# A hand-written opening order, y sums on TensorE and fp32 attention for a third block, in an attention and two-MoE kernel

## The chip, the cores and the metric

One core of a Trainium2 chip runs the whole kernel. The metric is device microseconds (us) from the first to the last instruction, as the median of three executions. Engines are named as the profile names them: PE is TensorE (PEld its weight loads), DVE is VectorE, ACT is ScalarE, POOL is GpSimd, and SP is the engine whose queue starts most DMAs. Each engine takes its instructions strictly in its own order and waits where one is not ready.

## The reference, cut

```python
# attention without softmax, then a dense two-layer block, then a mixture of 8 experts
kv  = einsum('bhsd,bhse->bhde', k, v)          # 8 batches, 8 heads, 576 rows, 64 columns
out = einsum('bhsd,bhde->bhse', q, kv)
x   = out / sqrt(mean(out*out, -1) + 1e-6) * g_norm      # 4608 tokens x 512
h   = x @ w_in                                           # 512 x 2048
g   = maximum(h, 0) + alpha * minimum(h, 0)
y   = g @ w_out                                          # 2048 x 512
e   = argmax(y @ w_gate, axis=1)
out = gate(y) * sigmoid(y @ w_output_gate)[e] * (relu(y @ w1[e]) @ w2[e])
```

The inputs of the dense block are 64 bits wide and are read as pairs of 32-bit words.

## The kernel before, in words

The 4608 tokens are 12 blocks of 384 (three tiles of 128). For every block there is an attention part that ends in `x`, the block's rows transposed, as an fp16 high and low part; then 16 pieces `h` (12 matmuls of 384 columns each, `h_piece`, L602), then three tiles `y` (48 matmuls of 512 columns each, `y_products`, L621). A product of split numbers is three fp16 matmuls: high by high, high by low, low by high. After each `h`, ACT scales it into `m` (L605), DVE makes `r` of it (L607), ACT writes the high half of `g` (L609) and POOL, in blocks 0 and 1, or DVE, in the later ones, the low half (L610).

The weights `wi` (of w_in) and `wo` (of w_out) are converted while blocks 0 and 1 run, in four quarters of four pieces each. A piece is a 0.5 MB load into one of five buffers, an absolute value on ACT (L454), then four DVE instructions that form an fp32 value from the two words (L455, L458, L460, L462: `build`). When a quarter's four pieces are built, a maximum over the 128 partitions is taken through two TensorE products (`all_max`, L150 and L155), a chain of small DVE instructions forms the scale (`pow2`, `scale_in`, `scale_out`), and each piece is split into a high part on ACT (L476) and a low part on DVE (L477). `h` of a quarter needs the four pieces of `wi`, `y` of a quarter the four of `wo`. Blocks 0 and 1 are therefore computed quarter by quarter (`h_part`, `y_part`), and the sums over quarters are kept in `accs` (in the buffers of `g` that are not yet in use): ACT scales the new quarter into `yt` (L660) and DVE adds it to the rescaled sum (L661).

The attention of blocks 0 and 1 is in fp32: ACT copies q (L318), PE transposes it (L321), ACT copies that to `qT` (L323), PE multiplies by `kvbd` into `ops` (L339). From block 2 on (`SPLIT_Q = 2`) q is scaled on POOL (L309), split into fp16 halves on ACT and DVE, transposed by a DMA, and multiplied by the split `kv16` (L336), whose scale comes from `kv_halves` (a scaling on POOL, L280). After `ops` the steps are the same: square (ACT, L341), sum (DVE, L343), a power on POOL (L350), an exponent by small DVE instructions (L353 to L362), scaling (DVE, L368), the high half on ACT (L372), the low half on POOL from block 2 on (L373), and a transposing DMA into `x` (L376).

The order on all engines is made by a scheduler that goes by its own estimates; only the last dense block and the expert part are pinned to the written order. After block 11 the routed rows go through the experts (L1090, L1112).

Of the kernel before, what the change touches and what calls it, by code (L numbers as in the profile page):

```python
# [20 lines left out]
P = 128  # L21
# [8 lines left out]
NG = 4  # L30
# [28 lines left out]
SPLIT_Q = 2  # L59
# [7 lines left out]
def body(ctx: ExitStack, tc, q, k, v, g_norm, w_in, w_out, alpha, w_gate, w_og, w1, w2, out):  # L67
# [60 lines left out]
    def pow2(am, nm, out_s, out_inv, top=14, wide=False):  # L128
# [111 lines left out]
    def load_kv_first():  # L240
        for nm, src, w in (("k", k, wi[:, 6:11]), ("v", v, wi[:, 11:16])):
# [3 lines left out]
            sp.dma_start(out=m, in_=src[0, :, 0:QJ * P, :].rearrange("h (p j) d -> p h j d", j=QJ))  # L245
            sp.dma_start(out=r, in_=src[0, :, QJ * P:S, :].rearrange("h p d -> p h d"))
            kv_in[nm + "r", 0] = r
            for n in range(NPAIR):
                kv_in[nm, n] = m[:, 2 * n:2 * n + 2]

    def kv_step(n):
# [19 lines left out]
    def kv_halves(b):  # L271
# [8 lines left out]
        pool.tensor_tensor(out=t, in0=src, in1=s_.unsqueeze(2).to_broadcast([P, H, D]), op=ALU.mult)  # L280
# [5 lines left out]
    def att_steps(i):  # L286
# [3 lines left out]
        split_q = i >= SPLIT_Q  # L290

        def tr(t):
# [3 lines left out]
            if split_q:  # L296
# [12 lines left out]
                pool.tensor_tensor(out=qs, in0=qv, in1=s_.unsqueeze(2).to_broadcast([P, H, D]), op=ALU.mult)  # L309
# [17 lines left out]
        def om(t):  # L327
# [987 lines left out]
```

## Time and profile before

| | |
|---|---|
| median of three runs | 1383.14 us (1381.43 to 1385.01) |
| the profiled execution | 1379.12 us |
| its span, first to last instruction | 1377.3 us |
| PE busy | 1274.2 us, 93% of the span |
| DVE busy | 837.6 us, 61% |
| ACT busy | 560.5 us, 41% |
| POOL busy | 334.0 us, 24% |
| mean granted TensorE clock | 0.965 of full speed |

Busy shares are averages over stages with different limits, so they are read by stage: the opening (blocks 0 and 1, with the weight conversion), blocks 2 to 11, and the experts. A group row gives a line of the kernel, engine, operation, what is written from what, the count, busy time and mean duration. A timeline row gives start and duration of one instruction or of several merged ones, and in brackets how long the engine had been idle and what it waited for. The granted clock has two levels, 2.4 GHz (1.0) and 1.2 GHz (0.5); a stretch's figure is a mean.

### The profile page before, as it was taken

What the parts mean: (1) busy time and instruction counts of PE and PEld (TensorE: products, weight loads), DVE (VectorE), ACT (ScalarE), POOL (GpSimd) and SP (SyncE); (2) the same over time, 40 slices, a digit from 0 to 9 for tenths busy, and PEclk for the clock granted to TensorE, in tenths of its full rate; (3) what the DMA queues carried; (4) which work ended last, traced back from release to release, by engine and by line L of the source; (5) the groups of instructions that cost most, each with busy time, mean ns of one, the idle gap of its engine ahead of it and who ended that gap; (6) DMA issues with size and microseconds to landing.
All of it is one profiled execution on the core that took longest, in us unless ns stands there. A gap on an engine that the chain in (4) does not pass through costs nothing. (4 is left out here: it accounts for less than half of the span.)

```text
span 1377.3 us, 21930 instructions
## 1 busy us (share of the span) xinstructions
PE 1274.2 (93%) x7586; PEld 659.5 (48%) x7586; DVE 837.6 (61%) x2476; ACT 560.5 (41%) x928; POOL 334.0 (24%) x410
## 2 busy tenths in 40 slices
PE   3579898899999999999999999999989999999995
PEld 2435354455555555555555555554434444444442
DVE  5989968777777887868696878562521221212210
ACT  3355553446554565655464656351111111111110
POOL 3023134332212222223231222101322221222210
PEclk9579998899999999999999999999999999999998
DMA  9944135547594867685736666316999799799641
GB/s 286 242 114 136 50 92 127 131 130 196 163 267 109 238 169 192 191 214 156 235 63 178 168 170 146 108 39 174 254 328 195 152 314 267 147 232 247 136 89 38
DMA packets 326433, 237.00 MB, mean 172 GB/s; under 512 B 249372, under 2 KB 282156, under 8 KB 321840
## 3 DMA queue, kind: packets, MB, share of 16 engines
q1 hardware_dynamic: 308144, 189.88, 55.6%
q0 software_dynamic: 8960, 28.91, 6.5%
q10 hardware_dynamic: 9216, 16.78, 3.8%
q8 instruction: 61, 1.00, 0.3%
q14 instruction: 52, 0.43, 0.1%
HBM read 248.34 MB, written 53.25 MB: 219 GB/s over the span
## 5 line engine op out<-in xcount | busy, mean ns | idle before, releaser
L602 PE MATMUL h<-x,wi 128*128 128x384 f16 x2304 | 410.3, 329 | 7.0 <-DMA x<-x 3.9
L621 PE MATMUL y<-wo,g 128*128 128x512 f16 x1728 | 408.0, 383 | 6.7 <-ACT g L609 3.5
L602 PEld LDWEIGHTS <-wi 128*128 128x128 f16 x2304 | 222.2, 98 | 163.0 <-issue 11.0
L621 PEld LDWEIGHTS <-g 128*128 128x128 f16 x1728 | 164.8, 98 | 192.9 <-issue 8.5
L1096 DVE CAST h_d<-br_d 128x512 f16<-128x512 f32 x62 | 26.7, 430 | 259.9 <-DMA hT_d<-h_d 147.3
L1112 PE MATMUL bo_d<-lane,hT_d 128*128 128x512 f16 x744 | 168.1, 383 | 7.8 <-DMA hT_d<-h_d 7.8
L1090 PE MATMUL bh_d<-lane,byT_d 128*128 128x512 f16 x744 | 165.3, 379 | 0.0
L609 ACT CAST g<-r 128x384 f16<-128x384 f32 x192 | 97.0, 508 | 113.3 <-DVE r L607 108.9
L607 DVE SCALAR_TENSOR_TENSOR r<-m,alphat 128x384 f32<-128x384 f32 x192 | 123.1, 642 | 23.5 <-ACT m L605 22.6
L1112 PEld LDWEIGHTS <-hT_d 128*128 128x128 f16 x744 | 73.0, 99 | 98.8 <-DMA hT_d<-h_d 9.3
L1090 PEld LDWEIGHTS <-byT_d 128*128 128x128 f16 x744 | 72.6, 98 | 88.1 <-issue 0.8
L350 POOL TENSOR_TENSOR rs<-ms,mhalf 128x8 f32<-128x8 f32 x36 | 67.3, 1869 | 192.8 <-DVE qm L353 192.7
L610 DVE TENSOR_TENSOR g<-r,g 128x384 f16<-128x384 f32 x160 | 91.7, 575 | 23.5 <-ACT g L609 22.8
L605 ACT ACTIVATE m<-h,scal 128x384 f32<-128x384 f32 x160 | 91.5, 574 | 27.8 <-PE h L602 26.5
L412 DVE SCALAR_TENSOR_TENSOR wlo_w<-rawe,es_w,whi_w 128x1024 f16<-128x1024 f32 x64 | 85.2, 1347 | 26.0 <-DMA ws<-wlo_w 15.8
L1094 ACT ACTIVATE br_d<-bh_d 128x512 f32<-128x512 f32 x62 | 37.0, 597 | 131.6 <-PE bh_d L1090 109.2
L763 POOL DMA_INDIRECT ytab<-row,pos x36 | 37.9, 1052 | 215.8 <-DVE pos L744 110.4
L542 ACT ACTIVATE eab_w<-rawe 128x1024 bf16<-128x1024 f32 x64 | 67.0, 1055 | 56.7 <-DMA rawe<-in_moe_w_dram 47.1
L411 ACT ACTIVATE whi_w<-rawe,es_w 128x1024 f16<-128x1024 f32 x64 | 71.3, 1144 | 31.9 <-DVE es_w L142 19.6
L1116 POOL DMA_INDIRECT out_dram<-ob_d,oidx_d x31 | 32.3, 1041 | 192.8 <-ACT ob_d L1115 192.8
L1115 ACT ACTIVATE ob_d<-bo_d,msc_d 128x512 f32<-128x512 f32 x31 | 21.3, 687 | 140.8 <-PE bo_d L1112 140.8
L373 POOL TENSOR_TENSOR x<-xs,x 128x512 f16<-128x512 f32 x30 | 37.2, 1241 | 105.0 <-ACT x L372 79.2
(363 smaller groups left out, 1366.7 us busy)
## 6 DMA issues: line engine op xcount, KB each, us to landing
lane<-ws SPq DMA_DIRECT2D x150, 1024.0 KB
rawe<-in_moe_w_dram SPq DMA_DIRECT2D x64, 512.0 KB
ws<-whi_w ACTq DMA_DIRECT2D x64, 256.0 KB
ws<-wlo_w SPq DMA_DIRECT2D x64, 256.0 KB
q<-in_q_dram SPq DMA_DIRECT2D x16, 512.0 KB
rawwi<-in_moe_w_in_dram SPq DMA_DIRECT2D x16, 512.0 KB
rawwo<-in_moe_w_out_dram SPq DMA_DIRECT2D x16, 512.0 KB
k<-in_k_dram SPq DMA_DIRECT2D x28, 256.0 KB
```

The lines of the kernel that those rows point to most:

```text
L350: pool.tensor_tensor(out=rs, in0=ms, in1=mhalf, op=ALU.pow)
L411: act.activation(out=dst_h, in_=src, func=AF.Copy, scale=s)
L412: dve.scalar_tensor_tensor(out=dst_l, in0=src, scalar=s, in1=dst_h, op0=ALU.mult, op1=ALU.subtract)
L542: act.activation(out=ab.rearrange("p a b -> p (a b)"), in_=raws[4 * m + i], func=AF.Abs)
L602: pe.matmul(ps, wi[:, f // 4 * NC + c, w, fs], xt[i][:, xc, :], start=(n == 0), stop=(n == 3 * NC - 1))
L605: act.activation(out=r0, in_=ps, func=AF.Copy, scale=(scst if start else scal)[:, f:f + 1])
L607: dve.scalar_tensor_tensor(out=r, in0=r0, scalar=alphat[:, f:f + 1], in1=r0, op0=ALU.mult, op1=ALU.max)
L609: act.copy(out=hi, in_=r)
L610: (pool if start else dve).tensor_tensor(out=lo, in0=r, in1=hi, op=ALU.subtract)
L621: pe.matmul(ps, g[:, t, f % GF, us], wo[:, f, w, :], start=(start and m == 0), stop=(stop and m == 2))
L1090: pe.matmul(hp[ts], j["yT"][:, x, ts], w1_[:, w, c, hs], start=(m == 0), stop=(m == 3 * NC - 1))
L1112: pe.matmul(po[ts], hT[:, g, ts], w2_[:, w, f, :], start=(m == 0), stop=(m == 3 * NFE - 1))
```

## The change

The first two blocks, up to the last `h` of block 1, stand in one hand-written order, pinned on PE, DVE, ACT and SP; before, the scheduler ordered them. `build` is cut into `magnitude` (ACT), `maximum` and `bits` (DVE) so that the pieces can be placed one by one. Each engine's rows before and after, at three places, follow the diff.

The sums of y over quarters move to TensorE: the old sum is multiplied by `keep`, a scaled identity in fp32, into the same PSUM tile (`y_unit`), and ACT copies the result out. The third block's attention takes the fp32 path (`SPLIT_Q = 3`), so `kv_halves` of batches 0 and 1 falls away. The copy of q is gone: PE transposes straight from the loaded tile, half a tile at a time. Three POOL steps go to DVE in all later blocks too: the scaling of q, of kv, and the low half of `x`. The early `kvbd` copies go from DVE to ACT. Maxima of one column need one DVE instruction less, the four small parameter loads start on ACT's queue, and the first k and v come in halves.

```diff
-SPLIT_Q = 2
+SPLIT_Q = 3
...
+    def max_rows(ps, n, nm):
         m = small.tile([E, 1], F32, tag="amrow", name="amrow" + nm)
         dve.tensor_reduce(out=m[:n], in_=ps[:n, 0:P], axis=AX.X, op=ALU.max)
+        if n == 1:
+            pe.matmul(ps[:, P:P + 1], ones32[:1, :], m[:1], start=True, stop=True)
+            return ps[:, P:P + 1]
...
-                dve.tensor_copy(out=kvbd[b % 2][sl, hp - 1:hp + 1, sl], in_=ps[sl])
+                (act.copy if b < 2 else dve.tensor_copy)(out=kvbd[b % 2][sl, hp - 1:hp + 1, sl], in_=ps[sl])
...
-        pool.tensor_tensor(out=t, in0=src, in1=s_.unsqueeze(2).to_broadcast([P, H, D]), op=ALU.mult)
+        dve.tensor_tensor(out=t, in0=src, in1=s_.unsqueeze(2).to_broadcast([P, H, D]), op=ALU.mult)
...
-                pool.tensor_tensor(out=qs, in0=qv, in1=s_.unsqueeze(2).to_broadcast([P, H, D]), op=ALU.mult)
+                dve.tensor_tensor(out=qs, in0=qv, in1=s_.unsqueeze(2).to_broadcast([P, H, D]), op=ALU.mult)
...
-                qj = scratch[(1, 2, 0, 3, 4, 5)[t]]
-                act.copy(out=qj.rearrange("p (h d) -> p h d", h=H), in_=qv)
-                qps = ps_a.tile([P, NPAIR, P], F32, tag="a", name="qps" + nm)
+                qps = (pool_ or ps_a).tile([P, NPAIR, P], F32, tag=tag, name="qps" + nm)
                 for hp in range(NPAIR):
-                    pe.transpose(qps[:, hp, :], qj[:, hp * P:(hp + 1) * P], ident)
+                    for e in range(2):
+                        pe.matmul(qps[64 * e:64 * e + 64, hp, :], qv[:, 2 * hp + e, :], ident, start=True, stop=True)
...
-            (dve if i < 2 else pool).tensor_tensor(out=x16[:, 1, :], in0=xs, in1=x16[:, 0, :], op=ALU.subtract)
+            tiles[t] = xs, x16
+
+        def low(t):
+            xs, x16 = tiles.pop(t)
+            dve.tensor_tensor(out=x16[:, 1, :], in0=xs, in1=x16[:, 0, :], op=ALU.subtract)
...
-            exp_to(ya[:, js], d[:, 0:1], 127 << 23)
-            exp_to(yb[:, js], d[:, 1:2], 127 << 23)
+            exp_to(d[:, 1:2], d[:, 1:2], 127 << 23)
+            act.activation(out=keep, in_=ident, func=AF.Copy, scale=d[:, 1:2])
...
+    def y_unit(i, j, g, acc, u):
+        ps = ps_y.tile([P, DM], F32, tag="y", name=f"y_{i}_{j}_{u}")
+        if j:
+            pe.matmul(ps, keep, acc[:, u, :], start=True, stop=False)
         for f in range(j * GF, (j + 1) * GF):
...
-                act.activation(out=t, in_=ps, func=AF.Copy, scale=ya[:, j:j + 1])
-                dve.scalar_tensor_tensor(out=acc[:, u, :], in0=acc[:, u, :], scalar=yb[:, j:j + 1], in1=t,
-                                         op0=ALU.mult, op1=ALU.add)
...
+        act.copy(out=acc[:, u, :], in_=ps)
...
+    with tc.manual_schedule(engines={ET.PE, ET.DVE, ET.Activation, ET.SP}):
+        load_kv_first(0)
...
+        din.magnitude(GF)
+        emit("i10 y000 i11 y001 i12 h100 i13 h101 r100 i14 h102 r101 i15 h103 r102 i16 y002 r103 i17 y100 i18 y101 o10 "
+             "y102 o11")
+        for j in range(1, NG):
+            emit(f"h0{j}0 o{j}2 h0{j}1 r0{j}0 o{j}3 h0{j}2 r0{j}1 o{j}4 h0{j}3 o{j}5 r0{j}2 h1{j}0 r0{j}3 o{j}6 h1{j}1 "
+                 f"r1{j}0 o{j}7 h1{j}2 r1{j}1 o{j}8 h1{j}3 r1{j}2")
...
+    for i in range(2):
+        for u in range(TB):
+            y_unit(i, NG - 1, gts[i], accs[i], u)
```

In the plan strings, `h0{j}x` is a piece of `h` of block 0 in quarter j, `r0{j}x` its `r` and `g`, `y0{j}u` a tile of `y`, `i` and `o` the steps of the conversion of `wi` and `wo` (0 to 3 build and take the maximum, 4 finishes the fourth piece, 5 is the second TensorE product, 6 the scale and high parts, 7 and 8 the low parts).

The first place is DVE in the first quarter, ahead of the low parts of `wi` (L477 before, L535 after). In the names, `x_0_2` is the third tile of block 0, `x_0_3` the first of block 1, `pw_ewi`, `sig`, `isig` and `scol` are the scale of `wi`. Before:

```order
L460 SCALAR_TENSOR_TENSOR cwo_1183<-rawwo_979,cwo_1183 128x512
L416 TENSOR_REDUCE amxwo_1236<-accwo_1123 128x1
L455 TENSOR_SCALAR uwi_1340,accwi_1339<-uwi_1340 128x512
L142 TENSOR_SCALAR sig<-isig 128x1
L373 TENSOR_TENSOR x_0_3_593<-xs_3_575,x_0_3_593 128x512
L486 TENSOR_TENSOR sig<-sig,sal 128x1
L487 TENSOR_TENSOR isig<-isig,ial 128x1
L488 TENSOR_TENSOR scol<-sig,gp 128x1
L132 TENSOR_SCALAR pw_ewg<-allmaxwg 128x1
L140 TENSOR_SCALAR kt<-pw_ewg 128x1
L142 TENSOR_SCALAR swg<-kt 128x1
L477 SCALAR_TENSOR_TENSOR wi<-wo,scol,wi 128x512 x2
```

After:

```order
L406 TENSOR_TENSOR x_0_1_450<-xs_1_384,x_0_1_450 128x512
L132 TENSOR_SCALAR pw_ewi_461<-allmaxwi_428 128x1
L135 TENSOR_SCALAR pw_ewi_461<-pw_ewi_461 128x1
L137 TENSOR_SCALAR sig<-pw_ewi_461 128x1
L139 TENSOR_SCALAR isig<-pw_ewi_461 128x1
L544 TENSOR_TENSOR scol<-sig,sgp 128x1
L545 TENSOR_TENSOR isig<-isig,ial 128x1
L406 TENSOR_TENSOR x_0_2_457<-xs_2_409,x_0_2_457 128x512
L508 TENSOR_SCALAR cwi_473<-uwi_402 128x512
L510 SCALAR_TENSOR_TENSOR cwi_473<-rawwi_250,cwi_473 128x512
L512 SCALAR_TENSOR_TENSOR wo<-rawwi_250,cwi_473 128x512
L535 SCALAR_TENSOR_TENSOR wi<-wo,scol,wi 128x512 x4
```

Block 1's attention and the builds of `wo` and of the second quarter of `wi` no longer stand ahead of the first low parts; the instructions of one build now follow each other directly.

The second place is the middle of the second quarter, where `y` of block 1 begins, on PE and DVE. `y_1_0` and `y_1_1` are tiles 0 and 1 of quarter 1; `allmaxwi` is the maximum for the third quarter of `wi`. PE after (before, no product by `keep` stands there):

```order
L686 MATMUL y_1_0_1312<-wo,g_200 128x512
L159 MATMUL allmaxwi_1289<-amrowwi_1327,ones_69 128x1
L711 MATMUL y_1_1_1343<-g_202,keep 128x512
L686 LDWEIGHTS g_200
L686 MATMUL y_1_1_1343<-wo,g_200 128x512
```

DVE before, in the second quarter:

```order
L477 SCALAR_TENSOR_TENSOR wo<-wi,sogs,wo 128x512
L460 SCALAR_TENSOR_TENSOR cwo_1504<-rawwo_1215,cwo_1504 128x512
L477 SCALAR_TENSOR_TENSOR wo<-wi,sogs,wo 128x512
L462 SCALAR_TENSOR_TENSOR wo<-rawwi_1187,cwi_1386 128x512
L477 SCALAR_TENSOR_TENSOR wo<-wi,sogs,wo 128x512
L152 TENSOR_REDUCE amrowwi_1412<-allmaxwi_1410 1x1
L477 SCALAR_TENSOR_TENSOR wo<-wi,sogs,wo 128x512
```

DVE after, at the third quarter's scale of `wi`:

```order
L512 SCALAR_TENSOR_TENSOR wo<-rawwi_1100,cwi_1306 128x512
L157 TENSOR_REDUCE amrowwi_1327<-allmaxwi_1289 1x1
L132 TENSOR_SCALAR pw_ewi_1330<-allmaxwi_1289 128x1
L135 TENSOR_SCALAR pw_ewi_1330<-pw_ewi_1330 128x1
L137 TENSOR_SCALAR sig<-pw_ewi_1330 128x1
L139 TENSOR_SCALAR isig<-pw_ewi_1330 128x1
L544 TENSOR_TENSOR scol<-sig,sgp 128x1
L545 TENSOR_TENSOR isig<-isig,ial 128x1
L535 SCALAR_TENSOR_TENSOR wi<-wo,scol,wi 128x512 x4
L500 TENSOR_SCALAR uwo_1341,accwo_1362<-uwo_1341 128x512
```

The scale chain now stands alone, behind a TensorE product that follows four tiles of `y`, and the low parts and the next builds stand behind it.

The third place is PE where block 2 begins. Before, the last rows of block 0's gate products (`l_2`) and its routing (`rk`) stand there, and nine rows of `rk` further on the first `h` of block 2:

```order
L697 LDWEIGHTS yT_2_2433
L697 MATMUL l_2_2468<-wg_148,yT_2_2433 128x32
L731 LDWEIGHTS tri_73
L731 MATMUL rk_2506<-oh_0_2498,tri_73 128x24
L733 LDWEIGHTS ones_71
L733 MATMUL rk_2506<-oh_0_2498,ones_71 128x16
```

After:

```order
L686 MATMUL y_3_2_2384<-wo,g_200 128x512
L273 MATMUL kvps_2_2173<-v_2_2149,k_2_2147 64x64 x8
L273 MATMUL kvps_2_2173<-vr_778,kr_774 64x64 x2
L273 MATMUL kvps_2_2173<-v_3_2168,k_3_2166 64x64 x8
L663 LDWEIGHTS wi
L663 MATMUL h_0_2405<-x_2030,wi 128x384
```

The second and third gate products and the routing of block 0 have moved behind the first pieces `h` of block 2.

## Rows read from the trace of the kernel before

**Rows 1.** Busy us (x instructions) by stretch: PE, PEld, DVE, ACT, POOL, PEclk, DMA share, GB/s

```profile
0.00:71.00 71.00, 32.77 (x287) 26.33 (x288) 51.80 (x181) 25.04 (x41) 12.52 (x54) 0.73 0.96 260
71.00:88.30 17.30, 12.05 (x62) 6.77 (x61) 15.13 (x58) 8.74 (x20) 9.09 (x8) 0.80 0.29 61
88.30:158.00 69.70, 61.58 (x299) 29.80 (x298) 68.84 (x162) 37.27 (x67) 15.23 (x13) 0.94 0.45 129
158.00:248.10 90.10, 76.65 (x503) 41.49 (x504) 71.86 (x227) 45.15 (x79) 31.51 (x28) 0.90 0.37 96
248.10:925.00 676.90, 662.30 (x4306) 360.91 (x4306) 523.23 (x1560) 369.94 (x604) 165.65 (x148) 1.00 0.61 163
925.00:1377.30 452.30, 428.81 (x2137) 194.20 (x2135) 106.73 (x293) 74.37 (x120) 100.03 (x161) 0.98 0.80 198
```

**Rows 2.** Timeline of DVE: start us, us, line, operation

```profile
15.28 0.69 DVE L455 TENSOR_SCALAR_CACHE_REDUCE uwi<-uwi 128x512 f32<-128x512 f32 x1
16.00 0.43 DVE L458 TENSOR_SCALAR cwi<-uwi 128x512 int32<-128x512 int32 x1
16.46 0.69 DVE L460 SCALAR_TENSOR_TENSOR cwi<-rawwi,cwi 128x512 int32<-128x512 int32 x1
17.07 0.68 DVE L455 TENSOR_SCALAR_CACHE_REDUCE uwi<-uwi 128x512 f32<-128x512 f32 x1
...
76.17 0.17 DVE L132 TENSOR_SCALAR pw_ekv<-allmaxkv 128x8 int32<-128x8 int32 x1 [1.60 <-PE allmaxkv L155]
76.37 0.17 DVE L140 TENSOR_SCALAR kvi<-pw_ekv 128x8 int32<-128x8 int32 x1
```

**Rows 3.** Timeline of the last v load's end on PE and of ACT, first loads

```profile
11.54 5.91 PE L262 MATMUL kvps<-wi 64*64 64x64 f32 x80 [11.54 <-DMA wi<-in_v_dram]
...
16.98 0.68 ACT L454 ACTIVATE uwi<-rawwi 128x512 f32<-128x512 f32 x1 [0.67 <-DMA rawwi<-in_moe_w_in_dram]
```

**Rows 4.** Timeline of PE, fp32 products of 128 columns (two records for each product)

```profile
19.97 1.13 PE L339 MATMUL ops<-kvbd,qT 128*128 128x128 f32 x8 [1.47 <-issue]
20.94 0.60 PE L321 MATMUL qps<-ident,g 128*128 128x128 f32 x4
...
41.23 2.08 PE L339 MATMUL ops<-kvbd,qT 128*128 128x128 f32 x8 [0.68 <-ACT qT L323]
```

**Rows 5.** Timeline where block 2's first `h` begins: SP's queue (SPq) and PE

```profile
244.79 1.24 SPq L376 DMA_TRANSPOSE x<-x  x1
...
246.36 0.20 PE L731 MATMUL rk<-oh,tri 128*128 128x24 f16 x1 [3.76 <-DVE oh L723]
...
248.09 7.00 PE L602 MATMUL h<-x,wi 128*128 128x384 f16 x24 [1.41 <-DMA x<-x]
```

**Rows 6.** Timeline of PE, `h` and `y` at the full clock

```profile
121.21 4.06 PE L602 MATMUL h<-x,wi 128*128 128x384 f16 x24
125.11 1.24 PE L621 MATMUL y<-wo,g 128*128 128x512 f16 x5
...
297.91 15.50 PE L621 MATMUL y<-wo,g 128*128 128x512 f16 x71
313.24 0.83 PE L336 MATMUL ops<-kv,qT 128*128 128x128 f16 x12
```

**Rows 7.** Timeline of POOL and DVE side by side

```profile
114.40 1.00 POOL L610 TENSOR_TENSOR g<-r,g 128x384 f16<-128x384 f32 x1 [3.94 <-ACT g L609]
114.54 1.41 DVE L460 SCALAR_TENSOR_TENSOR cwo<-rawwo,cwo 128x512 int32<-128x512 int32 x1
```

**Rows 8.** Groups of the first 248 us: the y sums on DVE

```profile
L661 DVE SCALAR_TENSOR_TENSOR g<-g,yb,yt 128x512 f32<-128x512 f32 x18 | 14.4, 800 | 6.5 <-ACT yt L660 6.5
```

**Rows 9.** Groups of the whole span on POOL

```profile
L350 POOL TENSOR_TENSOR rs<-ms,mhalf 128x8 f32<-128x8 f32 x36 | 67.3, 1869 | 192.8 <-DVE qm L353 192.7
...
L373 POOL TENSOR_TENSOR x<-xs,x 128x512 f16<-128x512 f32 x30 | 37.2, 1241 | 105.0 <-ACT x L372 79.2
L309 POOL TENSOR_TENSOR qs<-q,qsc 128x512 f32<-128x512 f32 x30 | 36.9, 1240 | 38.2 <-DVE qm L353 18.5 <-DVE qsc L142 11.8 <-DVE pw_er L132 3.6
```

More of the change, by code (lines that the diff above doesn't have):

```diff
@@ L1177, in body @@
-    prep = prep_in(0)
-    def prep_steps(n):
-        for _ in range(n):
-            if prep:
-                prep.pop(0)()
-    while prep:
-        prep_steps(1)
-        step(attq)
-        step(attq)
-    drain(attq)
-    for load in late:
-        load()
-    late = None
-    wgr = small.tile([P, NC, 2, E], F32, tag="wgr", name="wgr", bufs=1)
-    sp.dma_start(out=wgr[:, :, 0, :], in_=w_gate.rearrange("(c p) e -> p c e", p=P))
-    sp.dma_start(out=wgr[:, :, 1, :], in_=w_og.rearrange("(c p) e -> p c e", p=P))
+        load_kv_first(1)
@@ new lines, in top @@
+        def top(d, nm):
+            m = small.tile([P, 1], F32, tag="amx", name="amx" + nm)
+            dve.tensor_reduce(out=m, in_=d.acc, axis=AX.X, op=ALU.max)
+            return max_turn(m, nm, ps_l, "l")
+        (t0, t1, t2), tr, products, sums, exponents, scaled, low = att_parts(0)
+        din.magnitude(0)
+        for n in range(2):
+            kv_step(n)
+        din.build(0)
+        din.magnitude(1)
+        for n in range(2, NPAIR):
+            kv_step(n)
+        din.build(1)
@@ new lines, in body @@
+        for n in range(NPAIR, NPAIR + 2):
+            load_kv(n, True)
+        load_next()
+        tr(t0, ps_h, "h")
+        tr(t1, ps_h, "h")
+        while late:
+            late.pop(0)()
+        din.magnitude(2)
+        products(t0)
+        products(t1)
+        din.build(2)
+        tr(t2, ps_h, "h")
+        din.magnitude(3)
+        products(t2)
+        load_next()
+        sums(t0)
+        sums(t1)
+        din.maximum(3)
+        ps = top(din, "wi0")
+        sums(t2)
+        exponents(t0, t2)
@@ new lines, in body @@
+        ps = max_rows(ps, 1, "wi0")
+        scaled(t0)
+        scaled(t1)
+        low(t0)
+        scaled(t2)
+        low(t1)
+        scale_in(0, ps)
+        low(t2)
+        for i in range(3):
+            din.split(i, 0)
+        din.bits(3)
+        din.split(3, 0)
+        dout.magnitude(0)
+        load_next()
+        load_next()
+        (t3, t4, t5), tr, products, sums, exponents, scaled, low = att_parts(1)
+        tr(t3, ps_y, "y")
+        products(t3)
+        for n in range(NPAIR, NPAIR + 2):
+            kv_step(n, ps_y, "y")
@@ new lines, in body @@
+        while late:
+            late.pop(0)()
+        for i in range(GF):
+            din.split(i, 1)
+        load_next()
+        g = gts[0]
+        h0 = h_products(0, 0, True)
+        dout.build(0)
+        dout.magnitude(1)
+        h1 = h_products(0, 1, True)
+        h_unit(0, g, True, h0)
+        dout.build(1)
+        load_next()
+        dout.magnitude(2)
+        for n in range(NPAIR + 2, 2 * NPAIR):
+            kv_step(n)
+        tr(t4, ps_y, "y")
+        h_unit(1, g, True, h1)
@@ new lines, in body @@
+        h2 = h_products(0, 2, True)
+        tr(t5, ps_y, "y")
+        sums(t3)
+        dout.build(2)
+        load_next()
+        products(t4)
+        h3 = h_products(0, 3, True)
+        h_unit(2, g, True, h2)
+        dout.magnitude(3)
+        products(t5)
+        sums(t4)
+        dout.maximum(3)
+        ps = top(dout, "wo0")
+        sums(t5)
+        h_unit(3, g, True, h3)
+        exponents(t3, t5)
+        ps = max_rows(ps, 1, "wo0")
+        scaled(t3)
+        scaled(t4)
+        low(t3)
@@ L1195, in body @@
+        marks = {}
+        for ins in reversed(nc.cur_bb.bb.instructions):
+            if ins.engine in (ET.PE, ET.DVE, ET.Activation, ET.SP):
+                marks.setdefault(ins.engine, ins)
+    behind = ExitStack()
+    for ins in marks.values():
+        behind.enter_context(tc.issue_after(ins))
     gam = small.tile([P, 1], F32, tag="amx", name="gam")
```

340 lines of the change are left out of this document (204 added, 136 removed).

## The prediction

> **What bounds the kernel now.** I read the busy time by stretch first. Blocks 2 to 11 (248.1 to 925) keep PE busy for 662.3 of 676.9 us at a granted clock of 1.00, and the experts behind them 428.8 of 452.3 [rows 1]; DVE has 154 us to spare in the one and most of the other. Nothing but the 14.6 us in which PE idles can be won in blocks 2 to 11. The opening is another matter: up to 248.1 PE idles for 64.8 us (38.2, 5.2, 8.1 and 13.4 by stretch), and its granted clock is 0.73 and 0.80 up to the first `y` at 88.3. From 88.3 to 158 DVE is busy for 68.84 of 69.70 us: it sets the pace there. Ahead of it DVE shows 51.8 of 71, on a DMA share of 0.96. The timelines give three marks: the first `h` at 71.0, the first `y` at 88.3 (both are cuts of rows 1), block 2's first `h` at 248.09 [rows 5]. That `h` waited for a transposing DMA issued at 244.79, behind routing that had waited 3.76 us for DVE [rows 5]. So the sum is made of one question: when does block 2's first `h` come?
>
> **Step 1, the first h.** The change takes block 1's attention and the builds of `wo` out of DVE's queue ahead of the first low parts. One build is 0.72 + 0.46 + 0.61 + 0.69 by its starts, 2.5 us [rows 2]. The third raw block is on ACT at 16.98 [rows 3]; as much data stands ahead of it as before, the fourth lands some 3 us later. PE still gets its last v at about 11.5 and needs about 6 us for the first kv [rows 3]; transposes and products of three tiles cost four fp32 products of 128 columns each, 0.97 us at the full clock and 2.0 at half (eight records, four products, 2.08) [rows 4], so with ACT's copies between them the third tile's products end at about 29. Behind them on DVE: a sum and exponents, 2.0; a power on POOL, 1.87 [rows 9]; scalings and low parts of three tiles, about 4.5 (0.69 for a 128x512 step [rows 2]); which puts the last low part of `x` at about 38. The transposing DMA adds 3.3 (issued 244.79, usable 248.09) [rows 5]. The scale of `wi` is six small steps of about 0.2 (0.17 each and a gap) [rows 2], the fourth build 1.8, and one low part 0.69: 40.3, inside that. **The first h is at about 42** against 71.0; ends 38 (exponents hidden) and 50 (loads as late as DVE found them before).
>
> **Step 2, the first y.** What DVE was spared comes back: four builds of `wo` 10.0, block 1's three tiles 6.2 (three 0.69 steps each) with 16 small steps 2.7, four `r` 2.1 (0.69 x 384/512), the scale 1.4, four low parts 2.8; 25.2 us, and two waits for PE's maxima and ACT's high parts, 3. **70**, against 88.3.
>
> **Step 3, the quarters.** Before, 18 sums on DVE cost 14.4 us [rows 8]; they go. In their place PE gets 18 products by `keep`, fp32, 128x512. No such row exists; four times 128 columns gives 4 x 0.243 = 0.97 us at the full clock (estimate; 2.0 at half [rows 4]). That is 17.5 us more on PE, and it lies on the path wherever PE paces. From 70 PE has six `y` of 2.59 and twelve `h` of 1.95 [rows 6]: 38.9, with 2.6 for a clock not yet full 111.6. DVE has eight builds 20.0, twelve `r` 6.2, eight low parts 5.5, two scales 2.8, POOL's collisions 5.6 (below) and two waits of 2.2: 114.5. DVE is later, so quarter 1 is open to `y` at 114.5.
>
> A later quarter on PE: eight `h` 15.6 and six `y` with `keep` 6 x 3.56 = 21.4, together 37.0. On DVE it has two halves. The `o` half: three builds 7.5, the fourth's rest 1.8, four `r` 2.1, two maxima 1.1, the scale 1.7, ACT's high part 0.68, four more steps 3.2: 18.1. The `i` half does not run ahead, because its scale waits for a TensorE product that stands behind four tiles of `y` in the written order (4 x 3.56 = 14.2), then the scale 1.5, a high part 0.68 [rows 3], four low parts 2.8: 19.1. Queued behind that wait on DVE are the low parts and the next quarter's first builds; on ACT, `m` of the next `h` stands behind the high parts, and PE waits for its PSUM. Sum 37.2. While POOL makes a low half of `g` (1.00 us), a DVE step of 0.69 took 1.41 beside it [rows 7]: 0.7 lost per meeting, and six meetings a quarter in the `o` half give 41.4. I take 40, nearer to the meeting since rows 7 shows it in this very stage. Two quarters on, with 2.5 of extra small steps: the last quarter is open to `y` at 197.
>
> The Trainium skill's page "SBUF — State Buffer", section "Who interferes with whom", goes further: a DVE step with two SBUF inputs and a GpSimd step that reads SBUF exclude each other, and the later one stands still until the other has ended. The meeting in rows 7 (1.00 us of POOL, 0.72 us longer on DVE, begun 0.14 later) is a little short of that. By the page, eight meetings at up to 1.00 would make a quarter 18.1 + 8.0 + 19.1 = 45.2, 5.2 above the 40 taken, and the time 1375; the share that rows 7 shows gives 41.4 and 1368 at most. The result of the page's rule is the same as that of the strict chain below, and stands in its chance.
>
> **Step 4, the hand-over.** After 197 PE has six `y` with `keep`, 21.4; kv and the third block's three fp32 tiles stand between them: kv 3.5 (5.91 [rows 3] at the low clock), transposes 3.8, products 3.0; rest 1.2: 33. The last tile's chain beside it: products at 24, then square 0.7, sum 0.7, exponents 0.4, power 1.87 [rows 9], scaling, high and low part 2.0, transposing DMA 3.3 [rows 5]: 33 also. The routing of block 0, which stood ahead [rows 5], now follows. **Block 2's first h is at about 230** against 248.1, a gain of 18.
>
> **Step 5, blocks 2 to 11.** 27 scalings of q, 30 low halves of `x` and 6 scalings of kv leave POOL, where one takes 1.24 [rows 9], for DVE at 0.69: 63 x 0.69 = 43 us more, DVE 523 to 566 of 676.9 [rows 1]. Each also ends a meeting that cost DVE up to 0.7, so its true load may hardly grow. PE is the bound and has 14.6 us idle in all; the later work of routing is off its path. I take 0, ends -7 (half of the idle goes) and +6. If PE's cover were gone, the 43 would be the price. The copies of `kvbd` on ACT (8, about 0.3 each), the loads in halves and the parameter loads are hidden by ACT's idle and by the wait until 11.5: nothing.
>
> **The sum** against the profiled execution's 1379.12: 1361. The median of the runs is 4.0 above that execution, 1383.14, so 1365.
>
> **Rivals.**
> *PE paces the quarters.* POOL's meetings fall into DVE's waits. For it: DVE waits 14 us for the `i` half each time. Then quarters take 37.0 and the first begins at 111.6: 230 - 2 x 3 - 3 = 221, a time of 1356.
>
> *The conversion chain stays the bound and is strict.* A written order cannot use a gap: each PE wait for `ps_h` behind ACT's high parts is added to the next. For it: DVE's 68.84 of 69.70 [rows 1], when the scheduler filled it with anything. With all eight meetings a quarter is 18.1 + 5.6 + 19.1 = 42.8, with 1 us of waits 43.8, 3.8 above the 40; twice that and 2.4 in step 1 make 10: gain 8, 1375.
>
> *The opening does not come earlier.* The DMA share of 0.96 at 260 GB/s [rows 1] could hold the builds, and first `h` would stay near 60; the written order then only shifts its waits. Against it: ACT had the third block at 16.98 [rows 3]. Gain about 3: 1380.
>
> *Slower: DVE's new steps in blocks 3 to 11.* The 63 steps stand in DVE's queue among `r` (L607) and the low halves of `g` (L610), on which the next PE products wait. It decides once a block's DVE work, 52.3 us before and 56.6 after, comes in lumps that PE's `h`, 1.95 apart, cannot wait for: then up to half of the 43 is exposed. 1365 + 21.5 = 1387. Against it: 10 us of DVE a block stay free.
>
> **How the numbers follow.** Forecast 1365: 0.38. PE paces, 1356: 0.24. Strict chain, 1375: 0.20. Opening held, 1380: 0.08. Slower, 1387: 0.10. The range reaches down to 1347 (the PE rival with -7 of step 5 and a first `h` at 38) and up to 1382 (the held opening, or the forecast with the +6 of step 5 and a first `h` at 50). About 0.3%, 4.1 us, is what a measurement of this kernel can tell from no change: faster is below 1379.0, slower above 1387.3. Faster: the first three cases, 0.82. Same: the held opening, which lies at the bound, 0.08. Slower: the last, 0.10, which the range leaves out.
>
> **What would show it.** Step 1: the first `h` between 38 and 50 and low parts of `wi` right behind the fourth build. Step 2: the first `y` near 70. Step 3: a product by `keep` of about 0.97 us; from one quarter's first `y` to the next 40 us (37 with PE without gaps: the PE rival; 43 and more with PE waiting for ACT `m` or `wi`: the strict chain). Step 4: block 2's first `h` at 230. Step 5: from that to the experts 677 us with PE busy about 665; PE waiting for DVE `r` or `g` there speaks for the slower rival. A `keep` product of 2 us, or a low granted clock after the first `y`, would break the sum in step 3; an `x` that waits for the power on POOL, in steps 1 and 4.

## The result

The changed kernel takes 1392.55 us as the median of six runs (1390.87 to 1393.95), the kernel before 1384.89 in the same session: 1.0061 times as long, 95% interval 1.0047 to 1.0075. A second session gave 1395.1 against 1382.79, 1.0102 (1.0069 to 1.0135). One of the six executions of the kernel before took 1523.69 us and is left out of the ratio, which is worked out from the other single times and so differs a little from the quotient of the medians. The changed kernel is slower, by 0.6 to 1.0%, where I had forecast 1365 and faster. The profiled execution took 1392.6 with a span of 1390.6 us; that of before (1379.12) lay 4.0 to 5.8 us below the medians of its kernel (1383.14 and 1384.89), so the two profiles show 13.3 us where the medians show 7.7.

The busy time of the changed kernel by stretch, cut at the marks of the prediction (columns: length, then busy us and instructions of PE, PEld, DVE, ACT and POOL, granted clock, DMA share, GB/s):

```profile
0.00:42.60 42.60, 23.05 (x223) 19.46 (x223) 27.39 (x83) 14.50 (x25) 10.80 (x53) 0.83 0.94 255
42.60:68.80 26.20, 15.91 (x142) 10.67 (x141) 18.25 (x46) 11.67 (x24) 8.76 (x7) 0.83 0.39 114
68.80:118.20 49.40, 43.56 (x223) 22.01 (x223) 39.23 (x86) 25.82 (x48) 9.62 (x10) 0.93 0.54 147
118.20:166.30 48.10, 39.57 (x187) 19.46 (x187) 35.59 (x79) 21.29 (x39) 8.22 (x9) 0.96 0.27 88
166.30:213.70 47.40, 39.42 (x188) 19.42 (x187) 37.16 (x88) 21.78 (x39) 8.24 (x9) 0.96 0.16 51
213.70:247.40 33.70, 31.68 (x258) 17.88 (x257) 24.80 (x75) 16.04 (x28) 8.09 (x6) 1.00 0.58 157
247.40:932.90 685.50, 663.09 (x4364) 361.93 (x4365) 530.65 (x1642) 370.82 (x608) 96.00 (x90) 1.00 0.63 166
932.90:1390.60 457.70, 431.32 (x2144) 195.24 (x2141) 108.57 (x296) 74.97 (x121) 101.34 (x161) 0.97 0.80 196
```

These lines answer to [rows 1]. The first `h` now comes at 42.63 and the first `y` at 68.80, close to the forecast. Then two quarters take 48.1 and 47.4 us, with neither engine full: PE 39.6 and DVE 35.6 of 48.1, where DVE before had 68.84 of 69.70 [rows 1]. Block 2's first `h` comes at 247.4, no earlier to speak of than before [rows 5]. From there to the last block's first `y` it takes 685.5 us; before, 675.5 (248.09 to 923.62). What follows takes 457.7 against 453.7.

Set against the forecast's span these are the terms: 17.4 us of the opening that did not come (247.4, not 230), 10.0 in blocks 2 to 11 and 4.0 behind them. In which of them the 4.0 to 5.8 us lie by which the profiled execution of before was a quick one, a single profile of it does not show.

The quarter from 118.2 on PE (start, duration, and in brackets the idle time before and what ended it):

```profile
118.19 1.02 PE L711 MATMUL y<-g,keep 128*128 128x512 f32 x2
119.05 2.75 PE L686 MATMUL y<-wo,g 128*128 128x512 f16 x12
121.64 1.02 PE L711 MATMUL y<-g,keep 128*128 128x512 f32 x2
122.50 2.75 PE L686 MATMUL y<-wo,g 128*128 128x512 f16 x12
130.52 0.37 PE L152 MATMUL allmaxwi<-ident,amxwi 128*1 128x128 f32 x1 [5.27 <-DVE amxwi L1221]
130.69 1.92 PE L711 MATMUL y<-g,keep 128*128 128x512 f32 x2
132.39 3.52 PE L686 MATMUL y<-wo,g 128*128 128x512 f16 x12
135.75 1.02 PE L711 MATMUL y<-g,keep 128*128 128x512 f32 x2
...
139.29 0.38 PE L159 MATMUL allmaxwi<-amrowwi,ones 1*128 1x1 f32 x2
```

And the same quarter on DVE:

```profile
130.31 0.16 DVE L1221 TENSOR_REDUCE amxwi<-accwi 128x1 f32<-128x4 f32 x1
...
132.17 0.27 DVE L157 TENSOR_REDUCE amrowwi<-allmaxwi 1x1 f32<-1x128 f32 x1
139.71 0.16 DVE L132 TENSOR_SCALAR pw_ewi<-allmaxwi 128x1 int32<-128x1 int32 x1 [7.27 <-PE allmaxwi L159]
```

Read together, the two show a turn in which each engine stops for the other. The written order puts the first product of the maximum (L152) behind two tiles of `y`. PE has them done at 125.2, DVE is building weights until 130.3, and PE stands for 5.27 us although the four other tiles of `y` need nothing from that maximum. When it goes on, two more tiles stand ahead of the second product (L159), and now DVE stands for 7.27. PE also comes back slower: its granted clock is 0.51 from 130.5 to 134.0, near the level of 1.2 GHz, and 1.00 from there to 139.4. The next `keep` product and tile take 1.92 and 3.52 us in place of 1.02 and 2.75, 1.7 more.

### The profile page after: what moved, and what is told of

The parts are those of the page before. It is cut to its first block, busy times and chain, and to the rows that moved or that the text cites. A ratio compares the mean times of both kernels' runs of the same rounds, so it can differ in the third digit from the quotient of the medians.

```text
span 1390.6 us, 21985 instructions
## 1 busy us (share of the span) xinstructions
PE 1287.6 (93%) x7717; PEld 666.1 (48%) x7717; DVE 821.6 (59%) x2386; ACT 556.9 (40%) x931; POOL 251.1 (18%) x342
## 3 DMA queue, kind: packets, MB, share of 16 engines
q8 instruction: 62, 1.02, 0.3%
## 5 line engine op out<-in xcount | busy, mean ns | idle before, releaser
L672 DVE SCALAR_TENSOR_TENSOR r<-m,alphat 128x384 f32<-128x384 f32 x192 | 119.6, 625 | 30.1 <-ACT m L666 28.9
L675 DVE TENSOR_TENSOR g<-r,g 128x384 f16<-128x384 f32 x160 | 88.1, 551 | 15.3 <-ACT g L674 14.8
L455 DVE SCALAR_TENSOR_TENSOR wlo_w<-rawe,es_w,whi_w 128x1024 f16<-128x1024 f32 x64 | 81.0, 1278 | 20.8 <-DMA ws<-wlo_w 17.8
L675 POOL TENSOR_TENSOR g<-r,g 128x384 f16<-128x384 f32 x32 | 32.9, 1032 | 146.0 <-ACT g L674 146.0
```

The lines of the kernel that those rows point to most:

```text
L455: dve.scalar_tensor_tensor(out=dst_l, in0=src, scalar=s, in1=dst_h, op0=ALU.mult, op1=ALU.subtract)
L672: dve.scalar_tensor_tensor(out=r, in0=r0, scalar=alphat[:, f:f + 1], in1=r0, op0=ALU.mult, op1=ALU.max)
L675: (pool if start else dve).tensor_tensor(out=lo, in0=r, in1=hi, op=ALU.subtract)
```

## The experiments

**The two waits taken apart.** In e1_tiles_ahead the third and fourth tile stand ahead of both products:

```diff
-emit(f"i{n}0 {emit_y[0]} r1{j}3 i{n}1 {emit_y[1]} i{n}2 i{n}3 {emit_y[2]} i{n}4 {emit_y[3]} i{n}5 i{n}6 "
+emit(f"i{n}0 {emit_y[0]} r1{j}3 i{n}1 {emit_y[1]} i{n}2 {emit_y[2]} {emit_y[3]} i{n}3 i{n}4 i{n}5 i{n}6 "
```

> In the second and third quarter's turn to the next weights of wi, the third and fourth tile of y stand ahead of the two TensorE products of the maximum, no longer around them; nothing else is changed. Turn theory (PE stops 5.3 us after two tiles for DVE's maximum, then DVE stops 7.3 us for the second product behind two more tiles): both waits go, a quarter falls from 48 to about 41, block 2's first h from 247 to about 233, the time from 1392.5 to about 1379. Rival (DVE's own work of 36 us a quarter and its meetings with POOL set the pace, and the waits move to the other half): quarters stay at 46 or more, the time at 1389 or more.

Measured: 1377.09 us, 0.9968 of before (0.9942 to 0.9995). Its quarters by stretch, and its turn on PE:

```profile
120.10:161.50 41.40, 37.77 (x188) 19.15 (x186) 35.66 (x78) 21.26 (x39) 8.20 (x9) 1.00 0.30 102
161.50:204.10 42.60, 39.52 (x188) 19.77 (x188) 37.37 (x88) 21.77 (x39) 8.06 (x9) 0.96 0.18 59
204.10:237.90 33.80, 31.68 (x257) 17.89 (x257) 24.77 (x75) 15.98 (x28) 8.06 (x6) 1.00 0.59 154
```

```profile
131.26 2.75 PE L686 MATMUL y<-wo,g 128*128 128x512 f16 x12
133.85 0.27 PE L152 MATMUL allmaxwi<-ident,amxwi 128*1 128x128 f32 x1
134.49 0.38 PE L159 MATMUL allmaxwi<-amrowwi,ones 1*128 1x1 f32 x2 [0.37 <-DVE amrowwi L157]
```

Both waits are gone (0.37 is left), the first of the two quarters is 41.4 with the same DVE work (35.7) at a granted clock of 1.00, the second 42.6 at 0.96. The turn theory holds and its rival falls. The place of two small products in a row of six tiles is worth 11.5 us in these profiles (95.5 to 84.0 for the two quarters). Of this 9.5 arrive at block 2's first `h` (237.9), since the first quarter ended 1.9 later here. By the medians this version is 15.5 under the changed kernel, in another session. It is 0.3% under the kernel before, just clear of its interval.

**The next wait in the row.** e6_turn_later, on top of e1, moves the first product of `wo`'s maximum (step `o{j}3`) behind one more `h`; PE waits 2.23 us for it in e1. The second product (`o{j}5`) keeps its place, though the expectation speaks of both:

```diff
-h0{j}1 r0{j}0 o{j}3 h0{j}2 r0{j}1 o{j}4 h0{j}3
+h0{j}1 r0{j}0 h0{j}2 o{j}3 r0{j}1 o{j}4 h0{j}3
```

> On top of the tiles put ahead (e1_tiles_ahead), the two TensorE products of the maximum of w_out stand one piece h later, where PE waited 2.2 us for DVE. Turn theory: the wait of 2.2 goes in two or three quarters, a quarter falls from 41.4 to about 39, the time from 1377.1 to about 1372. Rival (at 41 the quarter is bound by DVE's chain of steps, and the 2.2 come back at the low parts of wo or at ACT's m): quarter 41, time within 2 us of 1377.

Measured: 1381.63, 0.9995 (0.9966 to 1.0024), no gain that can be told. PE's row of the first product in e1 shows the wait that was to go:

```profile
148.10 0.27 PE L152 MATMUL allmaxwo<-ident,amxwo 128*1 128x128 f32 x1 [2.23 <-DVE amxwo L1221]
```

PE's rows in e6 show what became of it:

```profile
146.44 0.27 PE L152 MATMUL allmaxwo<-ident,amxwo 128*1 128x128 f32 x1 [0.28 <-DVE amxwo L1221]
150.16 0.38 PE L159 MATMUL allmaxwo<-amrowwo,ones 1*128 1x1 f32 x2 [1.51 <-DVE amrowwo L157]
157.49 2.11 PE L663 MATMUL h<-x,wi 128*128 128x384 f16 x12 [0.99 <-ACT m L666]
159.44 1.02 PE L711 MATMUL y<-g,keep 128*128 128x512 f32 x2
```

The 2.23 became 0.28 and 1.51, and from one quarter's first `y` (118.40) to the next (159.44) it is 41.0. The quarter stays at 41, as the rival forecast. That DVE's chain is what bounds it is not shown, since most of the wait only went over to the second product, which had not moved; DVE is busy for 36.5 of the 41.0.

**The sums back on DVE** (e4_sums_dve): ACT copies the quarter out, DVE adds it.

```diff
-            pe.matmul(ps, keep, acc[:, u, :], start=True, stop=False)
...
+            act.copy(out=t, in_=ps)
+            dve.scalar_tensor_tensor(out=acc[:, u, :], in0=acc[:, u, :], scalar=keep[:, j:j + 1], in1=t, op0=ALU.mult,
+                                     op1=ALU.add)
...
```

> The sums of y over quarters are back on DVE: ACT copies the new quarter out and DVE adds it to the rescaled sum; no product by keep on PE. If the keep products (18 of about 0.86 us on PE) are what filled the quarters: 15 us less, 1377. Turn theory (the two waits on each other set the pace): PE is relieved by 5.2 us a quarter but DVE gets six steps of 0.7 to 1.4, so that the second product of the maximum comes about 1.7 earlier and all behind it later: 1391 to 1397.

Measured: 1402.69, 1.0143 (1.0102 to 1.0183), slower by more than either reading. PE in its second quarter:

```profile
115.43 5.34 PE L686 MATMUL y<-wo,g 128*128 128x512 f16 x24
129.08 0.37 PE L152 MATMUL allmaxwi<-ident,amxwi 128*1 128x128 f32 x1 [8.31 <-DVE amxwi L1225]
129.25 8.18 PE L686 MATMUL y<-wo,g 128*128 128x512 f16 x24
139.14 0.38 PE L159 MATMUL allmaxwi<-amrowwi,ones 1*128 1x1 f32 x2 [1.71 <-DVE amrowwi L157]
...
156.94 0.37 PE L152 MATMUL allmaxwo<-ident,amxwo 128*1 128x128 f32 x1 [7.26 <-DVE amxwo L1225]
...
172.64 5.34 PE L686 MATMUL y<-wo,g 128*128 128x512 f16 x24
```

The quarter is 57.2 us (115.43 to 172.64). Less work on PE only makes it wait longer, 8.3 and 7.3, and go slower behind the wait (24 matmuls in 8.18, not 5.34). Six steps of 0.74 stand in DVE's queue, and DVE waits 10.2 us in this quarter for ACT's copies that three of them need, ahead of the rest of a build and of the low parts. In this order `keep` on PE, 0.86 each by the starts (118.19 to 119.05), is the better way; the sums on DVE were not tried with the tiles of e1 put ahead.

**The third block in halves again.** e5_split2 sets `SPLIT_Q = 2` and scales kv of batches 0 and 1 at the hand-over; e7_split2_early puts these two scalings into DVE's wait of 7.3 us in the quarters:

```diff
-SPLIT_Q = 3
+SPLIT_Q = 2
...
+                elif what[0] == "k":
+                    kv_halves(int(what[1]) - 2)
...
-                emit(f"i{n}0 {emit_y[0]} r1{j}3 i{n}1 {emit_y[1]} i{n}2 i{n}3 {emit_y[2]} i{n}4 {emit_y[3]} i{n}5 i{n}6 "
+                emit(f"i{n}0 {emit_y[0]} r1{j}3 i{n}1 {emit_y[1]} i{n}2 i{n}3 {emit_y[2]} i{n}4 k{n}00 {emit_y[3]} i{n}5 i{n}6 "
```

> The third block's attention is split into fp16 halves again, as before the change, with its two scalings of kv; the rest is the changed kernel. If the fp32 path is worth something at the hand-over: block 2's first h comes 4 to 10 us later, behind two more chains of maxima, scalings and DMA transposes, 1396 to 1402. If the end of the opening hides them (PE still has six tiles of y with keep, 21 us): within 2 us of 1392.5.

> The third block's attention is split into fp16 halves as before the change, but the two scalings of kv that it needs stand in the second and third quarter's turn, where DVE of the changed kernel waits 7.3 us, and not at the hand-over (as in e5_split2, 1417.65). If those two chains at the hand-over were what cost e5 its 25 us: about 1392 or a little below, with block 2's first h at about 250 and blocks 2 to 11 at 668 to 675, since e5 had them at 667.5 from first to last r against 683.5. If the scalings of q and their transposing DMAs are the cost (that fp32 for the third block removes): still 1400 or more.

Measured: 1417.65, 1.0263 (1.022 to 1.0306), and 1403.5, 1.0164 (1.0141 to 1.0187). e5 lost more than either of its readings. From the last quarter's first `y` to block 2's first `h` it takes 64.5 us (213.67 to 278.18), where the changed kernel takes 33.7. With the scalings out of the way, e7 still takes 50.1 (217.70 to 267.76). PE there:

```profile
255.45 1.50 PE L348 MATMUL ops<-kv,qT 128*64 128x128 f16 x24 [6.19 <-DMA qT<-q]
...
267.76 6.03 PE L664 MATMUL h<-x,wi 128*128 128x384 f16 x24 [5.72 <-DMA x<-x]
```

The split path puts a transposing DMA of q between the load and the product, and at the hand-over nothing covers it. The second reading held for e7's time, and fp32 for the third block is worth some 9 to 14 us by the ratios (1.0164 against 1.0102 and 1.0061); the two scalings at the hand-over cost e5 another 14.

**The three moved steps.** e2_pool_back takes them back to POOL in the changed kernel, b1_moves_only makes them alone in the kernel before. This is one of the three lines as e2 has it (in e2 the low halves of block 2 stay on DVE):

```diff
...
-                dve.tensor_tensor(out=qs, in0=qv, in1=s_.unsqueeze(2).to_broadcast([P, H, D]), op=ALU.mult)
+                pool.tensor_tensor(out=qs, in0=qv, in1=s_.unsqueeze(2).to_broadcast([P, H, D]), op=ALU.mult)
...
```

> The three moved steps of the later blocks (scaling of q, scaling of kv, low half of x) are back on POOL from block 3 on; the rest is the changed kernel. If DVE's 60 new steps are what made blocks 2 to 11 longer (686 us from block 2's first h to the last block's first y, 675 before): these blocks fall by 8 to 10 us, the time to about 1384. If they cost nothing, because each step on DVE also ends a meeting with POOL (my prediction's term of 0): within 2 us of 1392.5, and the 8 to 10 us come from elsewhere or from one execution's chance.

> The kernel before with one part of the change alone: scaling of q, scaling of kv and low half of x on DVE in place of POOL. e2_pool_back took these back and lost 12 us. If the moves themselves gain (shorter chains to the transposing DMAs, no meetings of DVE with POOL): 6 to 12 us less than before, 1373 to 1379. If e2 lost by its interplay with the new opening's order: within 3 us of before, 1384.5. My slower rival (43 us more on DVE, half of it exposed): 1395 or more.

Measured: 1404.5, 1.0156 (1.0118 to 1.0194), and 1399.64, 1.0113 (1.0082 to 1.0144). Taking the moves back costs 9 to 12 us (against 1395.1 and 1392.55), so neither reading of the first expectation held; making them alone costs 17, which only the slower rival's number covers. Both profiles are the slowest of their kernel's runs (1414.35 and 1406.5), so the sizes below are too large by some of that. Blocks 2 to 11 by stretch, from block 2's first `r` to the last `r`: before,

```profile
252.80:924.50 671.70, 657.10 (x4290) 358.49 (x4289) 521.41 (x1559) 368.02 (x601) 163.29 (x147) 1.00 0.61 163
```

before with the moves (b1_moves_only),

```profile
258.30:944.90 686.60, 663.99 (x4289) 362.39 (x4287) 526.26 (x1616) 368.80 (x602) 91.02 (x91) 0.99 0.61 160
```

the changed kernel,

```profile
250.30:933.80 683.50, 661.09 (x4352) 360.58 (x4351) 529.72 (x1640) 370.82 (x608) 96.12 (x91) 1.00 0.63 165
```

and the changed kernel without them (e2_pool_back).

```profile
250.30:952.70 702.40, 673.05 (x4353) 366.20 (x4351) 534.43 (x1580) 373.02 (x609) 174.41 (x151) 0.97 0.61 161
```

One thing is plain. The moves put 57 more instructions on DVE in b1, and its busy time rises by 4.9 us, not by the 39 that 57 x 0.69 make; taken back in e2, 60 fewer instructions leave DVE 4.7 us busier. So they cost DVE hardly anything. What pays for them are DVE's other steps, which get shorter without POOL beside them. A low half of `q` and one of an expert's weights, before:

```profile
L313 DVE TENSOR_TENSOR q<-qs,q 128x512 f16<-128x512 f32 x25 | 20.4, 824 | 6.2 <-ACT q L312 6.2
L412 DVE SCALAR_TENSOR_TENSOR wlo_w<-rawe,es_w,whi_w 128x1024 f16<-128x1024 f32 x64 | 85.2, 1347 | 26.0 <-DMA ws<-wlo_w 15.8 <-ACT whi_w L411 9.9
```

and in b1:

```profile
L313 DVE TENSOR_TENSOR q<-qs,q 128x512 f16<-128x512 f32 x25 | 16.8, 684 | 0.1
L412 DVE SCALAR_TENSOR_TENSOR wlo_w<-rawe,es_w,whi_w 128x1024 f16<-128x1024 f32 x64 | 81.2, 1279 | 17.5 <-DMA ws<-wlo_w 15.2 <-ACT whi_w L411 1.9 <-issue 0.2
```

But the time is not DVE's busy time. PE's idle there is 14.6 before, 22.6 in b1, 22.4 after and 29.4 in e2: it rose by 8.0 and by 7.0, in both directions of the same edit. PE's busy time rose as well, by 6.9 and 12.0 for as many matmuls, at granted clocks of 0.99 and 0.97 in place of 1.00. The engines' order in blocks 2 to 11 comes from the scheduler, which sees other instructions after each of these edits. That the order is what makes the difference is an inference: no run kept it fixed while an edit was made.

**Is it one wait?** In the changed kernel PE waits longer for ACT's `m` in blocks 2 to 11. The waits (us in total, times, longest), with ACT's longest wait for DVE's scales, before:

```profile
ACT whi_w L411 <- DVE es_w L142: 19.6, 10, 4.5
PE h L602 <- ACT m L605: 1.6, 4, 0.9
```

and in the changed kernel:

```profile
ACT whi_w L454 <- DVE es_w L144: 40.5, 11, 9.5
...
PE h L663 <- ACT m L666: 7.6, 8, 2.1
```

ACT stands at a high part of an expert's weights for a scale that DVE forms late. e8_scale_tick forms it one background step earlier, on top of e1; e9_phase1 and e10_phase2, on top of e1 too, only shift the background steps by one and two pieces `h`:

```diff
-                yield
+                if i < 3:
+                    yield
...
             pow2(r, nm, s, inv)
+            yield
```

```diff
-            tick(f % 3 == 0)
+            tick(f % 3 == 1)
```

> On top of the tiles put ahead (e1, 1377.1): in blocks 2 to 10 the scale of each expert matrix is formed one step of the background work earlier, in the step of the last absolute value and no longer in that of the first high part. In the changed kernel and in e1 ACT stands 40 us in blocks 2 to 11 at a high part (whi_w) waiting for that scale (es_w), 19.6 in the kernel before; PE's wait for m, which ACT makes behind it, is 6 to 7.6 us against 1.6. If that is what made blocks 2 to 11 longer (683.6 from the first r of block 2 to the last, 671.7 before): ACT's wait under 10, PE's idle there from 22 to about 15, 1368 to 1372. Rival (any other order of the background work gives a time within some 10 us of it by chance, with the waits at other places): 1372 to 1390, no link with ACT's wait.

> On top of e1: in every block from the third on, the background step of the experts' weights is taken at the pieces h 1, 4, 7, 10, 13 and no longer at 0, 3, 6, 9, 12, 15; the same work, another order from the scheduler. If the order of blocks 2 to 11 alone is worth several us (theory for the 10 us that the changed kernel lost there): the span of these blocks moves by 4 us or more from e1's 683.7, either way. If it is the changed work that costs there: within 3 us of it.

> As e9_phase1, at the pieces h 2, 5, 8, 11 and 14. The same two readings: blocks 2 to 11 off 683.7 by 4 us or more, either way, if the order alone decides; within 3 us if the changed work does.

Measured: e8 1387.22, 1.002 (0.9994 to 1.0045); e9 1378.8, 0.9974 (0.9942 to 1.0005); e10 1380.3, 0.9983 (0.9947 to 1.0018). In e8 ACT's wait fell, though not under 10,

```profile
ACT whi_w L454 <- DVE es_w L144: 13.0, 9, 3.2
```

and the time rose by 7 us over e1 by the ratios, by 10 by the medians. PE's wait for `m` stayed at 6.4, as e1's 6.3. The kernel before with the moves (b1) says the same:

```profile
ACT whi_w L411 <- DVE es_w L142: 9.3, 8, 4.1
PE h L602 <- ACT m L605: 6.5, 4, 3.0
```

ACT waits less for the scale there than in the kernel before, and PE nearly as long for `m` as in the changed kernel. So ACT's wait is not what made these blocks longer. From first to last `r` the blocks took 693.7 in e8, 684.0 in e9 and 678.7 in e10, against 683.7 in e1. But these are single executions: that of e10 was the quickest of its ten (1368.77 by time), that of e8 the slowest (1394.53). By the letter of the two expectations e9 stays at e1's span and e10 leaves it by 5.0. By the medians e9 and e10 are 1.7 and 3.2 us over e1, so a shift of the background steps alone is not shown to matter, and only e8's order costs something.

**Chance or order?** r1_after_again is the changed kernel once more, e11_turn_phase2 joins e6 and e10.

> The changed kernel once more, unchanged, for a second profiled execution and more times. If the 12 us that blocks 2 to 11 took longer (683.5 from the first r of block 2 to the last, 671.7 before) belong to its order: 680 to 688 again and 1390 to 1394. If one execution's chance made them: 676 or less, and single times spread by more than 10 us.

> e6_turn_later and e10_phase2 together, as the version to keep: block 2's first h at about 235 as in e6, the time about 1377 to 1380 as each alone; below 1374 only if the two add up, which the theory that blocks 2 to 11 go by their order more than by their work doesn't promise.

Measured: 1395.1 for the first, with single times from 1390.68 to 1404.69. Its blocks 2 to 11:

```profile
254.00:940.60 686.60, 661.44 (x4352) 361.04 (x4351) 530.33 (x1640) 370.92 (x608) 94.75 (x91) 0.99 0.63 164
```

686.6 again, PE idle 25.2: the longer blocks belong to this kernel, not to one execution, though single times do spread by 14 us. e11 took 1377.2, 0.9957 (0.9926 to 0.9988), no better than e1 by the median, though its profiled execution reached block 2's first `h` at 230.8 and took 1369.5. Single times of e11 run from 1368.21 to 1384.02, of e1 from 1375.1 to 1386.52, so that the two cannot be told apart by these runs.

## Why the prediction was wrong, point by point

**Step 1, right in time, wrong inside.** The first `h` came at 42.63 (42 forecast). But the last low part of `x` was done at 34.1, not 38, and the low parts of `wi` at 38.5. What stood ahead of `h` was PE's own order: a product of block 1 that waited 6.62 us for ACT's `qT`, behind the high parts of `wi` in ACT's queue, and then 2.9 us of block 1's kv:

```profile
37.71 2.08 PE L350 MATMUL ops<-kvbd,qT 128*128 128x128 f32 x8 [6.62 <-ACT qT L334]
```

The sum hit its number by two errors of some 4 us each, which is luck. The 40.3 given beside it for the scale, the fourth build and a low part names no start; from 38 its terms give 41.7 (38 + 1.2 + 1.8 + 0.69), with no effect on the 42.

**Step 2, right in time, in part by luck.** First `y` at 68.80 (70 forecast), with one more stop of 1.71 behind the first matmul. DVE was to work 25.2 us and wait 3 between the two marks; it was busy for 18.3 and waited 8.8, 5.6 of them for ACT's first `m`. One build of `wo` was done ahead of the first `h`, and most low parts came behind the first `y`.

**Step 3, the step that failed.** Its terms were nearly right: a tile with `keep` takes 3.45 (3.56 forecast), eight `h` about 16 (15.6), and quarter 1 opened at 118.2 (114.5). A later quarter was to take 40 and took 48.1 and 47.4. Of the 17.4 us that the opening lacks, 13.0 lie in these two (95.5, against 80 and 2.5 of small steps), 4.9 in the first quarter (49.4, not 44.5), 0.7 in the hand-over, and the first `y` gave 1.2 back. I had seen that DVE's scale waits for a product behind four tiles and had put it down at 14.2 us of PE work without a gap. I did not see that an earlier product of the same maximum (L152) stands behind only two of these tiles and itself waits on DVE for three builds and the fourth's maximum, 12.1 us from the quarter's first `y` (118.19 to 130.31). So the term of 14.2 took 21.1 (118.19 to the second product at 139.29): PE's wait of 5.27 and 1.7 for its slower return make up the difference. The working let DVE's builds and PE's four tiles run side by side; the order made the engines take turns. Once that is undone (e1) the quarter is 41.4. That this is to the tenth the figure that the step had with six meetings is luck, since in e1 PE still waits 3.6 us in it, 2.2 of them for the maximum of `wo`.

The rival *conversion chain strict* had the right sign of this error with 43.8 a quarter, still too little. *PE paces* is excluded by PE's 39.6 of 48.1.

The meetings with POOL were sized well. The first of these rows of the changed kernel is the DVE step alone, the third the same step beside POOL:

```profile
151.44 0.61 DVE L672 SCALAR_TENSOR_TENSOR r<-m,alphat 128x384 f32<-128x384 f32 x1
...
152.67 0.91 POOL L675 TENSOR_TENSOR g<-r,g 128x384 f16<-128x384 f32 x1 [27.25 <-ACT g L674]
152.77 1.23 DVE L672 SCALAR_TENSOR_TENSOR r<-m,alphat 128x384 f32<-128x384 f32 x1
```

The meeting cost 0.62 us beside 0.91 of POOL; in this quarter five of POOL's eight steps met a DVE step and cost 3.4 in all (4.2 in the sum). Two of the five were steps with one input (L508), which took 1.18 us beside POOL in place of 0.43. The rule that the Trainium skill has in "SBUF — State Buffer", section "Who interferes with whom", that the later of the two stands until the other has ended, comes near to this row: by it DVE would end at 154.19 (152.67 + 0.91 + 0.61), and it ended at 154.00. The whole cost stayed far under what eight full meetings would make, since three met nothing.

**Step 4, right in size.** From the last quarter's first `y` to block 2's first `h` it took 33.7 (33). It began 17 us late.

**Step 5, right on DVE's load, wrong on the time.** The moved steps cost DVE about nothing, as shown. But I took 0 (-7 to +6) for blocks 2 to 11, and they took 10 more. Of the 11.8 between first and last `r` (671.7, 683.5), 4.0 are PE's busy time, with 62 more PE records, mostly kv and gate products that moved behind the mark; 7.8 are idle time, 22.4 against 14.6, and the wait for `m` alone grew by 6.0. The slower rival named the place but not the cause: DVE had no load to expose. Which feature makes the 7.8 is open: the moves, ACT's wait for the scale and the place of the background steps were tried, and none explains it by itself. One edit does take it away. With the third block in halves and the moves kept (e7) the idle is 12.7 and PE's wait for `m` 1.2, and from block 2's first `h` to the last block's first `y` it takes 675.5 us, as before the change. But the hand-over then costs 16 us more. In the changed kernel the longer blocks thus go with the fp32 path of the third block and the hand-over that it makes, while b1 has them without it; by what chain is not shown. Blocks 2 to 11 in a pinned order were not tried.

**The range** counted the opening's gain as safe in all cases but one; none of them had the opening faster to the first `y` and no faster at its end. Its two ends do not come out of the terms named for them either: 1356 - 7 - 4 is 1345, not 1347, and 1365 + 6 + 8 is 1379, under the 1380 of the held opening, not 1382. The measured time lies outside by either. PE's idle time up to 248.1, 64.8 in the reading of the bounds, adds up to 65.0; nothing rests on it.

## What to carry to other kernels

In an order written by hand, follow each small product of a scale or maximum round its whole turn, engine by engine, and put ahead of it as many tiles as its input takes to come; a bound made of each engine's own work leaves out the time in which two engines stop for each other. Where a scheduler orders the rest, an edit there changes the order too: undo it and do it alone before its price is believed, since here undoing an edit cost some 10 us, and doing it alone 17.

## What the runs showed of the hardware

After 5.27 us without work PE came back slower: a `keep` product and a tile took 5.44 us in place of 3.77, at a granted clock of 0.51 in the first 3.5 us. After 8.31 us in e4, 24 matmuls of `y` took 8.18 in place of 5.34 (granted clock 0.65), and after 7.26, 24 of `h` took 6.62 in place of 4.06 (0.61). In all three the wait cost about a third more than its own length. Behind waits of 2.23 in e1, 24 matmuls of `h` took 4.06 once (1.00) and 5.74 once (0.70), so for shorter waits these runs give no rule. The `keep` product, fp32, 128x512, took 0.86 us from its start to the next tile's, against the 0.97 of four products of 128 columns. And in a part that a scheduler orders, one edit and its reverse both raised PE's idle time, by 8 and by 7 us in some 680.
